# Expert results brought from columns back to rows by VectorE and a DRAM scratch in place of TensorE transposes

## The chip, the cores and the metric

The kernel runs on one core of a Trainium2 chip. Its engines work beside each other, each through its own queue in order: TensorE (PE, with its weight loads as PEld), VectorE (DVE), ScalarE (ACT), GpSimd (POOL) and SyncE (SP, which here only issues DMAs). The metric is the device time of one execution in microseconds, 367.65 us in the median of three runs of the kernel before.

## The reference

The input is q, k, v and forget logits of 4 sequences with 8 heads of 768 steps and 48 values. A gated linear attention comes first, then a mixture of 8 experts, of which each token uses one:

```python
f = 1.0 / (1.0 + np.exp(-f_logit))
for t in range(S):
    state = f[:, :, t, :, None] * state + np.einsum('bhd,bhe->bhde', k[:, :, t], v[:, :, t])
    y[:, :, t] = np.einsum('bhd,bhde->bhe', q[:, :, t], state)
x = y.transpose(0, 2, 1, 3).reshape(B * S, H * D)          # 3072 tokens of 384
logits = x @ w_gate
e_idx = np.argmax(logits, axis=1)
gate_w = softmax(logits)[np.arange(N), e_idx]
eom = 1.0 / (1.0 + np.exp(-(x @ w_output_gate)))
for e in range(E):                                         # 8 experts, 384 -> 1024 -> 384
    mask = e_idx == e
    ye = np.maximum(x[mask] @ w1[e], 0.0) @ w2[e]
    out[mask] = gate_w[mask, None] * eom[mask, e, None] * ye
```

## The kernel before

The first 126 us compute the attention, route each token and scatter its row of 384 values, with its number and 16 gate values behind it, into a DRAM list of its expert. What follows is the class `Experts`. The experts are taken by falling number of tokens, with capacities of 512, 448, 432, 416, 400, 400, 384 and 376 tokens, and are called expert 0 to 7 by that order.

Per expert, `mm1` (line 768) computes the hidden layer in eight f-steps of 128 hidden units: nine matmuls each, three input slices times three terms, since each factor is split into a high and a low part (`xh`, `xl`, `w1h`, `w1l`). ScalarE takes relu of the sum in PSUM as `hh` (line 783), and VectorE computes the rest `hl` from the same PSUM tile (line 784). This tile `h_ps` has two buffers, so f-step f+2 waits for `hl` of f-step f. `mm2` (line 791) is the second product. For experts 0 to 5 it has the weights of w2 stationary and the tokens as moving columns, so its result `y_ps` has the 384 output values on partitions, in three banks. `y_out` (line 822) copies the banks to SBUF, and `put` (line 829), called at f-steps 1 to 4 of the next expert's first product, turns one tile of 128 tokens by three TensorE transposes, lets ScalarE scale it by the token's gain and has POOL scatter the rows to the output by an indirect DMA. Experts 6 and 7, with three token tiles, use `mm2_rows` (line 805): there the tokens are stationary and w2 moves in 384 columns, so the result already has tokens on partitions. Expert 0 is done in two halves of 256 tokens, the first of them before the routing is known for all.

The order of the work on each compute engine is the order of the program, tied by `chain` (line 1086). So `run` (line 879) writes by hand what stands between the f-steps: the split of w2 into `w2h` on ScalarE and `w2l` on VectorE at even f-steps of the first product (line 632), and in the second product the splits of the next expert's w1, its three input slices (`x_in`, line 737: block transposes of 32 x 32 on VectorE, then `xh` and `xl`) and the thirteen small operations that compute the gains from the gate values `xm` (`gain_ops`, line 697). SP loads by expert: w1, the token blocks `xb`, `xm`, then w2 (lines 612 to 630 and 672), where each load waits for the split that frees its buffer.

Of the kernel before, what the change touches and what calls it, by code (L numbers as in the profile page):

```python
# [579 lines left out]
class Experts:  # L580
# [4 lines left out]
    def __init__(self, tc, nc, k, r, raw, right, w1, w2, xs_dram, out, kp):  # L585
        self.tc, self.nc, self.k, self.r, self.raw, self.right, self.kp = tc, nc, k, r, raw, right, kp
        self.w1, self.w2, self.xs, self.out = w1, w2, xs_dram.rearrange("(e n) w -> e n w", e=E), out
        k.gain = kp.tile([TS, NT, E], F32, name="gain")
        k.dst = kp.tile([TS, NT, E], I32, name="dst")

        self.first = kp.tile([TS, NT, RW], F32, name="first_x")
        self.apart, self.cleared, self.number = [], [], {}
        self.wr, self.whl, self.todo, self.gq = {}, {}, [], []
        self.xg, self.xb, self.xt, self.hs, self.ys, self.ysb = {}, {}, {}, {}, {}, {}
# [27 lines left out]
    def load_rest(self, s):  # L622
        e = self.number[s]
        if s > 0:
            self.blocks_in(s)
        for i in range(KF // 2):
# [5 lines left out]
    def split(self, m, s, i, eng=None):  # L632
        flat = lambda a: a.rearrange("p a b -> p (a b)")
        t = self.wr.pop((m, s, i))
        shape = [128, KC, 256] if m == 1 else [128, 2, DM]
        hi = self.wp.tile(shape, F32R, name=f"w{m}h")
        lo = self.wp.tile(shape, F32R, name=f"w{m}l")
        self.nc.scalar.copy(out=flat(hi), in_=flat(t))  # L638
        (eng or self.nc.vector).tensor_tensor(out=flat(lo), in0=flat(t), in1=flat(hi.bitcast(F32)), op=ALU.subtract)  # L639
        self.whl[m, s, i] = (hi, lo)  # L640


# [29 lines left out]
    def blocks_in(self, s):  # L672
# [7 lines left out]
        m = self.xp.tile([TS, NT, RW - DM], F32, name="xm")  # L680
# [3 lines left out]
        self.xb[s] = t[:, 0:nb, :]  # L684
        self.meta = getattr(self, "meta", []) + [(s, 0, nt, m)]

    def gains(self):

        kp = self.kp
        for s, j0, j1, t in self.meta:  # L690
            n = j1 - j0
            d, up, dn = (kp.tile([128, NT, E], F32, name=m)[:, 0:n] for m in ("g_d", "g_up", "g_dn"))
            mx, sm, so = (kp.tile([128, NT], F32, name=m)[:, 0:n] for m in ("g_mx", "g_sm", "g_so"))
# [3 lines left out]
    def gain_ops(self, s, j0, j1, t, d, up, dn, mx, sm, so):  # L697
# [4 lines left out]
        mine = k.perm[:, s, :] if s > 0 else self.r.top  # L702
        return [
            lambda: nc.gpsimd.tensor_scalar(out=k.dst[:, j0:j1, s], in0=t[:, 0:n, 0], scalar1=0.0,
# [86 lines left out]
    def mm2(self, s, f, part=0):  # L791

        wh, wl = self.whl[2, s, f // 2]
        hh, hl = self.hs[s, f][part]
        c0, n = sum(h[0].shape[1] for h in self.hs[s, f][:part]), hh.shape[1]
        for d in range(KC):
            if f == 0 and part == 0:
                self.ys[d] = self.psy.tile([128, 512], F32, name=f"y_ps{d}")
            ds = slice(d * 128, d * 128 + 128)
# [5 lines left out]
    def mm2_rows(self, s, step):  # L805

        k, nc = self.k, self.nc
        for j, n in self.rows(s):
            ps = self.psy.tile([128, 512], F32, name=f"y_ps{j}")
            i = 0  # L810
            for f in range(KF):
                wh, wl = self.whl[2, s, f // 2]
                hh, hl = (t[:, j * TS:j * TS + n] for t in self.hs[s, f][0])
                for a, b in ((hh, wh), (hl, wh), (hh, wl)):
                    nc.tensor.matmul(ps[0:n, 0:DM], a, b[:, f % 2, :], start=(i == 0), stop=(i == 3 * KF - 1))
                    i += 1
                step(j * KF + f)
            t = self.yp.tile([TS, DM], F32, name="o", bufs=3)
            nc.scalar.activation(out=t[0:n], in_=ps[0:n, 0:DM], func=AF.Copy, scale=k.gain[0:n, j, s:s + 1])
            self.scatter(s, j, n, t)  # L820

    def y_out(self, s):
        for d in range(KC):
            t = self.yp.tile([128, max(CAPS)], F32, name=f"y{d}")
            copy = self.nc.vector.tensor_copy if d == 1 else self.nc.scalar.copy
            copy(out=t[:, 0:CAPS[s]], in_=self.ys[d][:, 0:CAPS[s]])
            self.ysb[s, d] = t

    def put(self, s, j, n):
        ps = self.pso.tile([128, KC, 128], F32, name="o_ps")  # L830
        for d in range(KC):
            self.nc.tensor.transpose(out=ps[0:n, d, :], in_=self.ysb[s, d][:, j * TS:j * TS + n],
                                     identity=self.k.ident)
        t = self.yp.tile([TS, DM], F32, name="o", bufs=3)
        self.nc.scalar.activation(out=t[0:n], in_=ps[0:n].rearrange("p a b -> p (a b)"), func=AF.Copy,  # L835
                                  scale=self.k.gain[0:n, j, s:s + 1])
        self.scatter(s, j, n, t)

    def scatter(self, s, j, n, t):
        self.nc.gpsimd.indirect_dma_start(  # L840
# [38 lines left out]
    def run(self):  # L879
# [7 lines left out]
        for s in range(E):  # L887
# [33 lines left out]
            for f in range(KF):  # L921
# [6 lines left out]
                if s == 1:  # L928
                    step(1)
# [221 lines left out]
```

## Time and profile before

| what | value |
|---|---|
| median of three runs | 367.65 us (367.51 to 368.71) |
| profiled execution: time / span | 368.0 / 366.3 us |
| TensorE busy | 351.9 us, 96% of the span |
| VectorE busy | 245.9 us, 67% |
| ScalarE busy | 198.1 us, 54% |
| POOL busy | 146.2 us, 40% |
| SP's DMA queue | 56.82 MB in 58048 packets |

The span runs from the first to the last instruction of the profiled execution; the time of that execution is 1.7 us longer. Times in a timeline count from the span's start. A duration is what one instruction took from its start to its end. Matmuls are pipelined: the next one starts before the last has ended, so the distance of two starts says what one costs TensorE. The words in brackets behind a row are the idle time of the engine ahead of it and what ended it. The granted clock is TensorE's, in tenths of full speed on the page and as a fraction in the windows.

### The profile page before, as it was taken

What the parts mean: (1) busy time and instruction counts of PE and PEld (TensorE: products, weight loads), DVE (VectorE), ACT (ScalarE), POOL (GpSimd) and SP (SyncE); (2) the same over time, 40 slices, a digit from 0 to 9 for tenths busy, and PEclk for the clock granted to TensorE, in tenths of its full rate; (3) what the DMA queues carried; (4) which work ended last, traced back from release to release, by engine and by line L of the source; (5) the groups of instructions that cost most, each with busy time, mean ns of one, the idle gap of its engine ahead of it and who ended that gap; (6) DMA issues with size and microseconds to landing.
All of it is one profiled execution on the core that took longest, in us unless ns stands there. A gap on an engine that the chain in (4) does not pass through costs nothing. (4 is left out here: it accounts for less than half of the span.)

```text
span 366.3 us, 8386 instructions
## 1 busy us (share of the span) xinstructions
PE 351.9 (96%) x3121; PEld 327.0 (89%) x3121; DVE 245.9 (67%) x503; ACT 198.1 (54%) x468; POOL 146.2 (40%) x176
## 2 busy tenths in 40 slices
PE   8899999999998999999999999999999999999993
PEld 3678998888887899997999999999999999999993
DVE  6998989888994665666684585585575575666600
ACT  3576766866764652436634653554654654654510
POOL 6586796999989762001300220310210220242012
PEclk9999999999998999999999999999999999999999
DMA  8999999999548515976456456467366366331001
GB/s 258 348 359 356 338 223 257 297 262 252 174 121 269 206 74 158 254 244 150 136 177 125 168 180 134 137 192 160 129 197 154 129 196 154 131 103 58 2 23 43
DMA packets 61410, 67.09 MB, mean 183 GB/s; under 512 B 19106, under 2 KB 55989, under 8 KB 61360
## 3 DMA queue, kind: packets, MB, share of 16 engines
q1 hardware_dynamic: 58048, 56.82, 56.1%
q0 software_dynamic: 3312, 9.65, 7.3%
q8 instruction: 26, 0.43, 0.5%
q14 instruction: 24, 0.20, 0.2%
HBM read 53.53 MB, written 13.39 MB: 183 GB/s over the span
## 5 line engine op out<-in xcount | busy, mean ns | idle before, releaser
L840 POOL DMA_INDIRECT out<-o,dst x30 | 31.0, 1033 | 172.9 <-ACT o L835 87.5
L784 DVE SCALAR_TENSOR_TENSOR hl<-h_ps,hh 128x256 fp32r<-128x256 f32 (+6 forms) x72 | 39.2, 546 | 49.8 <-ACT hh L783 49.5
L779 PE MATMUL h_ps<-xh,w1h 128*128 128x400 f32 (+6 forms) x192 | 67.5, 351 | 0.8 <-ACT xh L733 0.5
L779 PE MATMUL h_ps<-xl,w1h 128*128 128x400 f32 (+6 forms) x192 | 65.1, 339 | 0.2 <-DVE xl L734 0.2
L779 PE MATMUL h_ps<-xh,w1l 128*128 128x400 f32 (+6 forms) x192 | 65.0, 338 | 0.0
L783 ACT ACTIVATE hh<-h_ps 128x256 fp32r<-128x256 f32 (+6 forms) x72 | 34.8, 483 | 49.3 <-PE h_ps L779 47.7
L801 PE MATMUL y_ps<-hh,w2h 128*128 128x256 f32 (+4 forms) x168 | 55.8, 332 | 0.0
L801 PE MATMUL y_ps<-hh,w2l 128*128 128x256 f32 (+4 forms) x168 | 55.6, 331 | 0.0
L801 PE MATMUL y_ps<-hl,w2h 128*128 128x256 f32 (+4 forms) x168 | 55.6, 331 | 0.0
L779 PEld LDWEIGHTS h_ps<-xh,w1h 128*128 128x128 f32 x192 | 36.1, 188 | 2.0 <-ACT xh L733 0.9
L779 PEld LDWEIGHTS h_ps<-xl,w1h 128*128 128x128 f32 x192 | 36.2, 188 | 0.9 <-DVE xl L734 0.5
L779 PEld LDWEIGHTS h_ps<-xh,w1l 128*128 128x128 f32 x192 | 36.0, 188 | 0.5
L226 POOL TENSOR_TENSOR q_t<-q_t,p 128x512 f32<-128x512 f32 x24 | 30.6, 1275 | 8.5 <-DVE p L212 5.6
L639 DVE TENSOR_TENSOR w2l<-w2r,w2h 128x768 fp32r<-128x768 f32 x31 | 30.7, 991 | 4.1 <-ACT w2h L638 1.9
L801 PEld LDWEIGHTS y_ps<-hh,w2l 128*128 128x128 f32 x168 | 31.6, 188 | 0.4
L801 PEld LDWEIGHTS y_ps<-hh,w2h 128*128 128x128 f32 x168 | 31.6, 188 | 0.4
L801 PEld LDWEIGHTS y_ps<-hl,w2h 128*128 128x128 f32 x168 | 31.6, 188 | 0.4
L248 PE MATMUL a_ps<-q_t,k_t 64*128 64x128 f32 x384 | 28.3, 285 | 3.7 <-POOL k_t L223 2.1
L212 DVE TENSOR_TENSOR_SCAN p<-f_ps,start_p 128x511 f32<-128x511 f32 x22 | 28.0, 1273 | 3.7 <-ACT start_p L200 2.1
L639 DVE TENSOR_TENSOR w1l<-w1r,w1h 128x768 fp32r<-128x768 f32 x28 | 26.9, 960 | 4.0 <-ACT w1h L638 2.5
L248 PEld LDWEIGHTS a_ps<-q_t,k_t 64*128 64x128 f32 x384 | 23.6, 187 | 6.5 <-POOL k_t L223 2.5
L223 POOL TENSOR_TENSOR k_t<-k_t,i 128x512 f32<-128x512 f32 x21 | 27.0, 1285 | 4.2 <-DVE i L219 2.7
(176 smaller groups left out, 739.1 us busy)
## 6 DMA issues: line engine op xcount, KB each, us to landing
w1r<-in_w SPq DMA_DIRECT2D x32, 384.0 KB, 4.0
w2r<-in_w SPq DMA_DIRECT2D x32, 384.0 KB, 3.1
xs_dram<-empty SPq DMA_DIRECT2D x8, 401.0 KB, 11.8
f_t<-in_f SPq DMA_DIRECT2D x6, 512.0 KB, 3.9
q_t<-in_q SPq DMA_DIRECT2D x6, 512.0 KB, 9.4
k_t<-in_k SPq DMA_DIRECT2D x6, 512.0 KB, 9.6
v_t<-in_v SPq DMA_DIRECT2D x6, 512.0 KB, 8.9
v_t<-in_v SPq DMA_DIRECT2D x4, 768.0 KB, 14.5
```

The lines of the kernel that those rows point to most:

```text
L212: nc.vector.tensor_tensor_scan(out=flat(d["p"])[:, 1:n], data0=flat(d["f"])[:, 0:n - 1], data1=sp[:, 1:n], initial=sp[:, 0:1], op0=ALU.mul ...
L223: eng.tensor_tensor(out=k_t[i][:, :, sl], in0=k_t[i][:, :, sl], in1=d["i"], op=ALU.mult)
L226: nc.gpsimd.tensor_tensor(out=q_t[i][:, :, sl], in0=q_t[i][:, :, sl], in1=d["p"], op=ALU.mult)
L248: nc.tensor.matmul(aps[t][par][:, g, :], k_t[b % 2][r, g, sl], q_t[b % 2][r, g, sl], start=(g == 0), stop=(g == NP - 1))
L639: (eng or self.nc.vector).tensor_tensor(out=flat(lo), in0=flat(t), in1=flat(hi.bitcast(F32)), op=ALU.subtract)
L779: nc.tensor.matmul(ps[:, 0:n], a[:, c, cs], b, start=(i == 0), stop=(i == 3 * KC - 1))
L783: nc.scalar.activation(out=hi, in_=ps[:, 0:n], func=AF.Relu)
L784: nc.vector.scalar_tensor_tensor(out=lo, in0=ps[:, 0:n], scalar=0.0, in1=hi.bitcast(F32), op0=ALU.max, op1=ALU.subtract)
L801: self.nc.tensor.matmul(self.ys[d][:, c0:c0 + n], a[:, f % 2, ds], b, start=(f == 0 and i == 0 and part == 0), stop=(f == KF - 1 and i == ...
L840: self.nc.gpsimd.indirect_dma_start(out=self.out, out_offset=bass.IndirectOffsetOnAxis(ap=self.k.dst[0:n, j, s:s + 1], axis=0), in_=t[0:n] ...
```

## The change

Expert 0 computes its second product by rows. Its four token tiles use the three banks in turn, and ScalarE scales each tile out of its bank. Experts 1 to 5 keep tokens as columns, but the split of w2 permutes the output values, so that each 32 partitions of a bank hold one contiguous quarter of the row. VectorE then turns each bank by one instruction of 32 x 32 block transposes out of PSUM, scales all three by the gain, and SP writes the result in four DMAs to a DRAM scratch and reads it back with tokens on partitions; POOL scatters from there. These steps stand in the list `back`, one of which is taken per f-step of the next expert's first product (three transposes, scaling, store, an empty step, fetch, first scatter), the rest in its second product. The gains of experts 1 to 5 are computed on 32-token blocks, four times over in the partitions, so that `xm` is loaded by four DMAs, and the token numbers come by a load of their own (`who`). The loads of w2 are issued after f-step 5 in place of ahead of the first product. The three result banks are allocated once. The scatters to the output no longer wait for one another.

```diff
+        self.yps = [self.psy.tile([128, 512], F32, name=f"y_ps{d}") for d in range(KC)]
...
+        if m == 2 and self.turned(s):
+            shape = [128, KC, 2 * 128]
+            flat = lambda a: a.rearrange("p d (x j) -> p d x j", j=SB)
+            t = t.rearrange("p a w -> p (a w)").rearrange("p (x d j) -> p d x j", d=KC, j=SB)
...
+        raw = t if m == 2 and self.turned(s) else flat(t)
-        self.nc.scalar.copy(out=flat(hi), in_=flat(t))
-        (eng or self.nc.vector).tensor_tensor(out=flat(lo), in0=flat(t), in1=flat(hi.bitcast(F32)), op=ALU.subtract)
+        self.nc.scalar.copy(out=flat(hi), in_=raw)
+        (eng or self.nc.vector).tensor_tensor(out=flat(lo), in0=raw, in1=flat(hi.bitcast(F32)), op=ALU.subtract)
...
+        return s > 0 and len(self.rows(s)) > KC
...
+        if self.turned(s):
+            for b in range(128 // SB):
+                self.nc.sync.dma_start(
+                    out=m[SB * b:SB * b + SB, 0:nb, :],
+                    in_=self.xs[bass.ds(e, 1), 0:nb * SB, DM:RW].rearrange("o (a t) w -> t (o a) w", t=SB))
+            self.who[s] = self.xp.tile([TS, NT, 1], F32, name="who")
+            self.nc.sync.dma_start(
+                out=self.who[s][:, 0:nt, :],
+                in_=self.xs[bass.ds(e, 1), 0:nt * TS, DM:DM + 1].rearrange("o (j p) w -> p (o j) w", p=TS))
+            self.meta = getattr(self, "meta", []) + [(s, 0, nb, m)]
+            return
...
-                self.nc.tensor.matmul(self.ys[d][:, c0:c0 + n], a[:, f % 2, ds], b,
-                                      start=(f == 0 and i == 0 and part == 0), stop=(f == KF - 1 and i == 2),
-                                      skip_group_check=True)
...
+                self.nc.tensor.matmul(self.yps[d][:, 0:n], a[:, d, fs], b, start=(f == 0 and i == 0),
+                                      stop=(f == KF - 1 and i == 2), skip_group_check=True)
+    def mm2_row(self, s, j, n, f):
+        ps = self.yps[j % KC]
+        wh, wl = self.whl[2, s, f // 2]
+        part, c0 = (j * TS // EARLY, j * TS % EARLY) if s == 0 else (0, j * TS)
+        hh, hl = (t[:, c0:c0 + n] for t in self.hs[s, f][part])
+        for i, (a, b) in enumerate(((hh, wh), (hl, wh), (hh, wl))):
+            self.nc.tensor.matmul(ps[0:n, 0:DM], a, b[:, f % 2, :], start=(f == 0 and i == 0),
+                                  stop=(f == KF - 1 and i == 2))
...
+    def turn_back(self, s):
+        nb = -(-CAPS[s] // SB)
+        yt = self.yp.tile([128, SLOTS // SB, BW], F32, name="yt")
+        ys = self.yps
+        def turn(d):
+            self.nc.vector.transpose(out=yt[:, 0:nb, SB * d:SB * d + SB],
+                                     in_=ys[d][:, 0:nb * SB].rearrange("p (a j) -> p a j", j=SB))
+        ob = self.yp.tile([128, SLOTS // SB, BW], F32, name="ob")[:, 0:nb, :]
+        def scale():
+            self.nc.vector.tensor_tensor(out=ob, in0=yt[:, 0:nb, :],
+                                         in1=self.k.gain[:, 0:nb, s:s + 1].broadcast_to([128, nb, BW]), op=ALU.mult)
+        rows = self.yd[s]
+        def store():
+            for b in range(128 // SB):
+                self.nc.sync.dma_start(
+                    out=rows[0:nb * SB, BW * b:BW * b + BW].rearrange("(a t) w -> t a w", t=SB),
+                    in_=ob[SB * b:SB * b + SB])
+        t = self.yp.tile([TS, NT, DM], F32, name="yr")
+        full = CAPS[s] // TS
+        def fetch():
+            self.nc.sync.dma_start(out=t[:, 0:full, :], in_=rows[0:full * TS].rearrange("(j p) w -> p j w", p=TS))
+            if CAPS[s] % TS:
+                self.nc.sync.dma_start(out=t[0:CAPS[s] % TS, full, :], in_=rows[full * TS:CAPS[s]])
+        def put(j, n):
+            self.other_rows(self.nc.gpsimd.indirect_dma_start(
+                out=self.out, out_offset=bass.IndirectOffsetOnAxis(ap=self.k.dst[0:n, j, s:s + 1], axis=0),
+                in_=t[0:n, j, :], in_offset=None, bounds_check=N - 1, oob_is_err=False))
+        self.back = ([lambda d=d: turn(d) for d in range(KC)] + [scale, store, lambda: None, fetch]
+                     + [lambda j=j, n=n: put(j, n) for j, n in self.rows(s)])
+    def backs(self, n=1):
+        for _ in range(min(n, len(self.back))):
+            self.back.pop(0)()
+    def other_rows(self, i):
+        for other in self.results:
+            self.tc.declare_no_dep(i.ins, other.ins, reason="other tokens")
+        self.results.append(i)
...
-            self.mm2(0, f)
+            for j, n in self.rows(0)[0:EARLY // TS]:
+                self.mm2_row(0, j, n, f)
+        self.back = []
...
-                self.load(s + 1, self.k.number[0:1, s + 1:s + 2])
-            back = self.rows(s - 1) if s > 0 and len(self.rows(s - 1)) > KC else []
+                self.load(s + 1, self.k.number[0:1, s + 1:s + 2], rest=False)
+                self.blocks_in(s + 1)
...
-                if 1 <= f <= len(back):
-                    self.put(s - 1, *back[f - 1])
+                self.backs(1)
+                if f == 5 and s > 0 and s + 1 < E:
+                    self.load_w2(s + 1)
...
+            if not self.turned(s):
+                if s == 0:
+                    for j, n in self.rows(0)[0:EARLY // TS]:
+                        self.row_out(0, j, n)
+                def beside(i):
+                    self.backs(1)
+                    if front and (i % 2 if s == 0 else i % 3 == 1):
+                        front.pop(0)()
+                    else:
+                        self.gain(1)
+                self.mm2_rows(s, EARLY // TS if s == 0 else 0, beside)
+                while front:
                     front.pop(0)()
-                self.gain(2)
-                if s == 1:
-                    step(1)
+            else:
+                for f in range(KF):
+                    self.mm2(s, f)
+                    if front:
+                        front.pop(0)()
+                    self.gain(2)
+                    self.backs(2)
+                    if s == 1:
+                        step(1)
...
-            self.y_out(s)
+            self.backs(len(self.back))
+            if self.turned(s):
+                self.turn_back(s)
```

## Rows read from the trace of the kernel before

**Rows 1.** The page, part 1, and the granted clock of part 2.

```profile
PE 351.9 (96%) x3121; PEld 327.0 (89%) x3121; DVE 245.9 (67%) x503; ACT 198.1 (54%) x468; POOL 146.2 (40%) x176
...
PEclk9999999999998999999999999999999999999999
```

**Rows 2.** TensorE's timeline, expert 2: start, duration, line, operands, count.

```profile
195.63 0.36 PE L779 MATMUL h_ps<-xh,w1h 128*128 128x432 f32 x1
...
197.37 0.36 PE L779 MATMUL h_ps<-xh,w1h 128*128 128x432 f32 x1
...
199.11 0.49 PE L832 MATMUL o_ps<-ident,y 128*128 128x128 f32 x3
199.35 0.44 PE L779 MATMUL h_ps<-xh,w1h 128*128 128x432 f32 x1
...
201.19 0.49 PE L832 MATMUL o_ps<-ident,y 128*128 128x128 f32 x3
```

**Rows 3.** Groups by line and shape: busy us, mean ns, idle before.

```profile
L639 DVE TENSOR_TENSOR w2l<-w2r,w2h 128x768 fp32r<-128x768 f32 x31 | 30.7, 991 | 4.1 <-ACT w2h L638 1.9
...
L638 ACT CAST w2h<-w2r 128x768 fp32r<-128x768 f32 x32 | 26.5, 827 | 0.0
...
L832 PE MATMUL o_ps<-ident,y 128*128 128x128 f32 x57 | 9.5, 274 | 0.0
...
L784 DVE SCALAR_TENSOR_TENSOR hl<-h_ps,hh 128x448 fp32r<-128x448 f32 x8 | 5.0, 622 | 5.4 <-ACT hh L783 5.3
...
L742 DVE STREAM_TRANSPOSE xc<-xb 128x448 f32<-128x448 f32 x6 | 4.5, 749 | 0.0
...
L713 DVE RECIPROCAL g_dn<-g_dn 128x32 f32<-128x32 f32 x6 | 2.1, 344 | 0.0
...
L734 DVE TENSOR_TENSOR xl<-xc,xh 128x448 fp32r<-128x448 f32 x3 | 1.9, 625 | 1.9 <-ACT xh L733 1.9
```

**Rows 4.** Timeline of ScalarE, first group of expert 2.

```profile
197.57 0.53 ACT L783 ACTIVATE hh<-h_ps 128x432 fp32r<-128x432 f32 x1 [1.21 <-PE h_ps L779]
197.99 0.82 ACT L638 CAST w2h<-w2r 128x768 fp32r<-128x768 f32 x1
```

**Rows 5.** Timeline of VectorE, the same place.

```profile
198.13 0.61 DVE L784 SCALAR_TENSOR_TENSOR hl<-h_ps,hh 128x432 fp32r<-128x432 f32 x1 [2.28 <-ACT hh L783]
198.85 0.96 DVE L639 TENSOR_TENSOR w2l<-w2r,w2h 128x768 fp32r<-128x768 f32 x1
```

**Rows 6.** Windows: span, busy PE, PEld, DVE, ACT, POOL, clock, DMA share, GB/s.

```profile
155.57:164.02 8.45, 8.45 (x74) 8.45 (x73) 5.15 (x12) 3.42 (x8) 0.00 (x0) 1.00 0.70 238
195.63:210.91 15.28, 15.28 (x86) 14.57 (x84) 7.61 (x12) 9.03 (x16) 3.01 (x3) 1.00 0.52 136
```

**Rows 7.** Timeline of TensorE, expert 7's second product by rows.

```profile
349.57 0.34 PE L815 MATMUL y_ps<-w2h,hh 128*128 128x384 f32 x1
...
351.69 0.34 PE L815 MATMUL y_ps<-w2h,hh 128*128 128x384 f32 x1
```

**Rows 8.** Timeline of VectorE before expert 1's input is turned.

```profile
156.92 0.96 DVE L639 TENSOR_TENSOR w1l<-w1r,w1h 128x768 fp32r<-128x768 f32 x1 [0.30 <-DMA w2r<-in_w]
157.79 0.18 DVE L706 TENSOR_REDUCE g_mx<-xm 128x4 f32<-128x32 f32 x1
```

**Rows 9.** Timeline of TensorE, first group of expert 1.

```profile
165.03 0.36 PE L779 MATMUL h_ps<-xh,w1l 128*128 128x448 f32 x1
165.89 0.47 PE L779 MATMUL h_ps<-xh,w1h 128*128 128x448 f32 x1 [0.50 <-ACT xh L733]
166.55 0.47 PE L779 MATMUL h_ps<-xl,w1h 128*128 128x448 f32 x1 [0.19 <-DVE xl L734]
```

**Rows 10.** DMA issues of SP for expert 1.

```profile
148.86 1.71 SPq L681 DMA_DIRECT2D xm<-xs_dram  x1
```

**Rows 11.** Timeline of POOL at the same time.

```profile
155.10 0.25 POOL L704 TENSOR_SCALAR dst<-xm 128x4 int32<-128x4 f32 x1 [11.74 <-DMA xm<-xs_dram]
```

**Rows 12.** The page, part 3, SP's queue.

```profile
q1 hardware_dynamic: 58048, 56.82, 56.1%
```

More of the change, by code (lines that the diff above doesn't have):

```diff
@@ L622, in load_rest, with load_w2 @@
     def load_rest(self, s):
-        e = self.number[s]
         if s > 0:
             self.blocks_in(s)
+        self.load_w2(s)
+    def load_w2(self, s):
+        e = self.number[s]
         for i in range(KF // 2):
@@ L702, in gain_ops @@
         mine = k.perm[:, s, :] if s > 0 else self.r.top
+        number, nt = (self.who[s], len(self.rows(s))) if self.turned(s) else (t, n)
         return [
-            lambda: nc.gpsimd.tensor_scalar(out=k.dst[:, j0:j1, s], in0=t[:, 0:n, 0], scalar1=0.0,
+            lambda: nc.gpsimd.tensor_scalar(out=k.dst[:, 0:nt, s], in0=number[:, 0:nt, 0], scalar1=0.0,
                                             scalar2=float(BIG), op0=ALU.max, op1=ALU.min),
@@ L789, in mm1_early, with mm2 @@
         self.mm1(0, f, True)
-    def mm2(self, s, f, part=0):
+    def mm2(self, s, f):
         wh, wl = self.whl[2, s, f // 2]
-        hh, hl = self.hs[s, f][part]
-        c0, n = sum(h[0].shape[1] for h in self.hs[s, f][:part]), hh.shape[1]
+        hh, hl = self.hs[s, f][0]
+        n, fs = hh.shape[1], slice((f % 2) * 128, (f % 2) * 128 + 128)
         for d in range(KC):
-            if f == 0 and part == 0:
-                self.ys[d] = self.psy.tile([128, 512], F32, name=f"y_ps{d}")
-            ds = slice(d * 128, d * 128 + 128)
@@ L800, in mm2 @@
             for i, (a, b) in enumerate(((wh, hh), (wl, hh), (wh, hl))):
-                self.nc.tensor.matmul(self.ys[d][:, c0:c0 + n], a[:, f % 2, ds], b,
-                                      start=(f == 0 and i == 0 and part == 0), stop=(f == KF - 1 and i == 2),
-                                      skip_group_check=True)
[L805 to L833, printed above, removed]
+                self.nc.tensor.matmul(self.yps[d][:, 0:n], a[:, d, fs], b, start=(f == 0 and i == 0),
+                                      stop=(f == KF - 1 and i == 2), skip_group_check=True)
@@ L834, in put, with mm2_rows @@
         t = self.yp.tile([TS, DM], F32, name="o", bufs=3)
-        self.nc.scalar.activation(out=t[0:n], in_=ps[0:n].rearrange("p a b -> p (a b)"), func=AF.Copy,
+        self.nc.scalar.activation(out=t[0:n], in_=self.yps[j % KC][0:n, 0:DM], func=AF.Copy,
                                   scale=self.k.gain[0:n, j, s:s + 1])
         self.scatter(s, j, n, t)
+    def mm2_rows(self, s, j0, step):
+        for j, n in self.rows(s)[j0:]:
+            for f in range(KF):
+                self.mm2_row(s, j, n, f)
+                step((j - j0) * KF + f)
+            self.row_out(s, j, n)
@@ L916, in run @@
             self.gains()
-            if len(self.rows(s)) <= KC:
-                self.mm2_rows(s, lambda i: self.gain(1) if i % 3 != 1 else front.pop(0)() if front else None)
-                self.gain(len(self.gq))
-                continue
-            for f in range(KF):
-                for part in range(len(self.hs[s, f])):
-                    if not (s == 0 and part == 0 and f < AHEAD):
-                        self.mm2(s, f, part)
-                if front:
-                    front.pop(0)()
-                self.gain(2)
-                if s == 1:
-                    step(1)
+            if not self.turned(s):
[10 more added lines that the diff above has]
+                while front:
+                    front.pop(0)()
+            else:
+                for f in range(KF):
+                    self.mm2(s, f)
[5 more added lines that the diff above has]
+                        step(1)
             self.gain(len(self.gq))
-            self.y_out(s)
+            self.backs(len(self.back))
+            if self.turned(s):
+                self.turn_back(s)
             if s == 0:
@@ L1089, in tile_kernel @@
     y_dram = dram.tile([H, D, N], F32, name="y_dram")
+    yd = [dram.tile([SLOTS, DM], F32, name=f"yd{s}") for s in range(E)]
     kp = ctx.enter_context(tc.tile_pool(name="const", bufs=1))
@@ L1096, in tile_kernel @@
         right = cx.enter_context(ExitStack())
-        ex = Experts(tc, nc, k, r, raw, right, w1, w2, xs_dram, out, kp)
+        ex = Experts(tc, nc, k, r, raw, right, w1, w2, xs_dram, out, kp, yd)
         with ExitStack() as c1:
```

24 lines of the change are left out of this document (14 added, 10 removed).

## The prediction

> **What bounds the kernel now.** I read the page first: TensorE is busy 96% of the span at a granted clock of 0.9 in all slices but one [rows 1], so what matters is what stands in its queue, and where it waits. The timeline of TensorE in expert 2's first product comes next [rows 2]. Eight groups of nine matmuls follow one another every 1.74 us (195.63 to 197.37). Where three transposes of the previous expert's result stand between two groups, the spacing is 2.08 (199.11 to 201.19): 0.24 for the transposes, and 0.10 more because the group's first matmul starts late. So a transposed row tile costs TensorE 0.34 us, and no wait is hidden in it. The whole-run groups [rows 3] give the prices of VectorE and ScalarE, and two timelines [rows 4, 5] show how an f-group hands over to them. The windows by stage [rows 6] show that VectorE has room in expert 2's first product (7.6 of 15.3 us busy), but not how that room lies, which decides this change.
>
> **What goes.** Experts 0 to 5 have four row tiles each, so 24 tiles with three transposes (57 full ones in [rows 3], the rest narrower ones at the same price): 24 x 0.34 = 8.2 us of the critical engine. This is at most 8.6 and at least 24 x 0.24 = 5.8, if the late first matmul stays. The ScalarE copies and scalings that go with them were beside TensorE and give nothing by themselves.
>
> **Expert 0 by rows.** Its second product was 144 matmuls of 256 columns, 8.45/72 = 0.117 us apiece [rows 6]. It becomes 96 of 384 columns, which experts 6 and 7 already do at (351.69 - 349.57)/12 = 0.177 [rows 7]: 16.9 becomes 17.0 in the second-half price, while the first half ran at 0.120. I take a gain of 0.1 (between -0.4 and +0.2).
>
> **What comes to VectorE in the first product of experts 2 to 6.** In f-steps 0 to 2 one block transpose each of 448 or 416 columns, in step 3 one scaling of 14 x 96 = 1344 or 13 x 96 = 1248 elements. A block transpose of 448 from SBUF takes 0.749 [rows 3]; I take 0.75 (0.70 for 416). The scaling is priced on w2l, 0.99 in the mean and 0.96 when undisturbed for 768 elements [rows 3, 5], with (0.96 - 0.622)/(768 - 448) = 1.06 ns per further element from it and hl of 448 columns: 1.57 and 1.47 us. Bounds: the transpose 0.62 to 1.24 (one or two plain passes of hl's length), the scaling 1.4 to 3.
>
> VectorE is in order, and the next hl (the low half of the hidden values) stands behind these. PSUM has two buffers for the first product, so group f+2 can't start until hl of group f is done. Before, hl ended at 198.13 + 0.61 = 198.74, for a group due at 199.11: 0.37 us of slack only [rows 2, 5]. I follow the hand-over for expert 2 from the start of group 0, with these steps: ScalarE's hh starts 0.20 after a group's last issue slot and hl 0.56 later [rows 4, 5], w2h follows 0.42 behind hh and is ready after 0.86, and a VectorE instruction lets the next start 0.08 before its own end (156.92 to 157.79 for one of 0.96 [rows 8]); I allow 0.05 from hl to the group that it releases.
> Step 0: hl ends at 3.1, w2l runs 3.2 to 4.1, the transpose to 4.8. Step 1: hl waits for it and ends at 5.40; group 3 was due at 5.22 and starts at 5.45, 0.23 late. The transpose runs to 6.0, hl of step 2 to 6.6, w2l 6.7 to 7.6, the transpose to 8.3. Step 3: hl ends at 8.88, just in time for group 5 at 8.93; the scaling runs to 10.3. Step 4: hl ends at 10.89 and group 6, due at 10.67, starts 0.27 late. Then the lag is gone. That is 0.50 us. The same steps with the shorter spacings of experts 3 to 6 (9 x 0.187, twice 9 x 0.180, 9 x 0.174) give 0.63, 0.62, 0.62 and 0.76: together 3.1 us. With the cheapest values (0.62, 1.4) they give 1.7, with a transpose of 1.24 they give 9.5, with a scaling of 3 they give 10.0.
> [...]
>
> **The permuted split of w2.** w2h and w2l of experts 1 to 5 read their input in runs of 32 columns. The element count stays, so I see no gain; the dearest near row is the block transpose, which reads every third element and takes 0.749 against 0.622 for a plain pass of as many columns: 1.2 times [rows 3]. At 1.2 the stalls are 5.1, at twice the price 19.6 and 2.5 more in expert 1. I take 1.0, since runs of 32 are nearer to plain reading.
>
> **Gains on 14 columns in place of 4.** For experts 1 to 5 four VectorE operations per expert grow from 32 to 112 elements (0.08 each by the slope above), and the reciprocal from 0.344 to at most 1.2 in proportion [rows 3]; I take 0.8. Some 1.0 us per expert lies in the second product, where VectorE ends its part 2 us ahead of TensorE; covered for experts 2 to 5, and if that cover went it would cost up to 1 us each. For expert 1 it isn't covered: these operations now come to stand between its last xl (then about 165.9) and its first hl, 2.1 us of them, so hl ends near 168.7 with group 2 due at 168.35: +0.4 (0 to +1).
>
> **The start of expert 1.** TensorE waits there for xh and xl: group 0's matmuls start at 165.89 and 166.55 in place of about 165.23 and 166.1, 1.1 us in all [rows 9]. In the new order x_in 2 has five gain operations ahead of it in place of eight, but the split before it starts 1 us later, since two scalings of expert 0's rows go ahead on ScalarE. I get the last xl 0.5 us earlier: -0.4 (-1.1 to +1).
>
> **What is moved on SP.** The xm load becomes four of the same size plus a column of 4-byte elements. The old xm was issued at 148.86 and released POOL at 155.10 [rows 10, 11]; VectorE first reads it at 157.79 [rows 8]. The queue's packets cost 0.561 x 16 x 366.3/58048 = 0.057 engine-us each on average [rows 12], so 3 x 448 more packets take at most 4.8 us and less in proportion to bytes: landing between 155.4 and 160, while the first read is now due near 158.9. I take no cost; late by 1.1 at most by this, 2 if SP's issue of 1.71 repeats. In later experts the load is issued over 15 us ahead. The w2 loads go behind the store, some 5 us later than now, 15 us ahead of their use. Store, fetch and the scatters behind the fetch hold up SP and POOL alone; the next w1 loads behind the fetch have a first product's length of cover. The last of it, expert 5's, is out during expert 6, so the tail stays. The kept banks are free long ahead: expert s's transposes run at most 9 us into the next first product, whose second product writes them 5 us later.
>
> **Sum.** -8.2 + 3.1 - 0.1 + 0.4 - 0.4 = -5.2 us. The profiled execution took 368.0 (span 366.3), which becomes 362.8; it lay 0.35 above the median of 367.65, so the median becomes 362.4. What is late next is VectorE's hl in the first products.
>
> **Rivals.**
> A, the back transposes hide. For it: VectorE is busy only half of that stage [rows 6]. Against it: the slack of a single hl is 0.37. With 1.7 of stalls and the wait of expert 1 gone: -8.2 + 1.7 - 0.1 - 1.1 = -7.7, 359.9.
> B, VectorE becomes the bound and the kernel slower. The place is the first product, the price the permuted split at 1.5 times (1.44 on VectorE, 1.23 on ScalarE): my steps then give 10.3 us of stalls, and 0.7 in expert 1: -8.2 + 11.0 - 0.1 = +2.7, 370.3. It decides from a split of about 1.35 times, or a transpose of 1.15 us, on: 8 us of stalls. Against it are the rows on plain and strided reading [rows 3]. [...]
> C, the enlarged xm lands late for expert 1 and VectorE, in order, holds x_in behind it: +2 us, 364.4. For it: DMA queues are the only thing with no cover there; against it the sum of packets.
> D, the two shares cancel: with a split at 1.2 times and a transpose of 1.0 the steps give 8.7 of stalls: -8.2 + 8.7 - 0.1 + 0.4 - 0.4 = +0.4, 368.0.
>
> **Chances.** My forecast 0.62 (its own range 360.5 to 364.7), A 0.12, C 0.06, D 0.07, B 0.13. About 0.3% (1.1 us) is what a measurement of this kernel tells from no change. Faster: 0.62 + 0.12 + 0.06 = 0.80; same 0.07; slower 0.13. The range 359.3 to 367.5 leaves out B, most of D and a little of A.
>
> **What would show it.** Right: no transposes by identity in the first products; spacing of 1.74 in expert 2 apart from two late groups released by hl, some 0.2 us each; block transposes near 0.75 and a scaling near 1.5 on VectorE; w2l still 0.96. Wrong: w2l or w2h above 1.2 us, block transposes above 1 us, a wait of VectorE for xm before 160, or TensorE idle in second products.

## The result, and the profile of the changed kernel

The changed kernel takes 361.61 us in the median of four runs (361.12 to 366.17), against 367.75 for the kernel before on the same chip: 0.985 of its time (95% interval 0.981 to 0.989), or 6.1 us less. The forecast was 362.4, with 5.2 us less. The profiled execution took 361.12 us, with a span of 359.4 against 366.3.

The page of the changed kernel, part 1 and the granted clock, answers to [rows 1]:

```profile
PE 343.4 (96%) x3001; PEld 317.6 (88%) x3001; DVE 259.4 (72%) x517; ACT 183.2 (51%) x436; POOL 146.8 (41%) x176
...
PEclk9999999999999999999999999999999999999999
```

A 9 on the clock's line stands for 0.9 or more, and not for 0.9 as the prediction reads it: the windows below, before and after, have 1.00 in every stage.

TensorE has 120 instructions and 8.5 us of work less, VectorE 13.5 us more. TensorE's share of the span stays at 96%, so the page doesn't yet say whether the new VectorE work is hidden. The windows do, if one cuts them at the first matmul of each stage. For the first products of experts 1 to 6, the changed kernel (columns as in [rows 6]):

```profile
163.01:178.87 15.86, 15.22 (x73) 13.37 (x73) 10.76 (x21) 7.88 (x14) 2.79 (x3) 1.00 0.78 189
193.41:207.81 14.40, 14.40 (x73) 13.28 (x72) 9.95 (x15) 6.61 (x11) 0.00 (x0) 1.00 0.61 97
221.73:235.79 14.06, 14.05 (x73) 13.21 (x72) 9.79 (x15) 6.52 (x11) 0.94 (x1) 1.00 0.61 135
249.23:262.91 13.68, 13.66 (x73) 12.95 (x73) 9.45 (x15) 6.43 (x11) 1.01 (x2) 1.00 0.61 137
276.03:289.71 13.68, 13.66 (x74) 12.94 (x73) 9.46 (x15) 6.44 (x11) 1.86 (x2) 1.00 0.63 155
302.86:316.18 13.32, 13.23 (x74) 12.43 (x74) 9.27 (x15) 6.35 (x11) 0.45 (x1) 1.00 0.46 116
```

The kernel before, the same stages but for expert 2, which stands in [rows 6]:

```profile
164.02:181.09 17.07, 16.38 (x86) 14.56 (x85) 10.68 (x21) 10.15 (x18) 3.01 (x3) 1.00 0.63 165
...
224.83:239.63 14.80, 14.80 (x86) 14.46 (x85) 7.45 (x12) 8.93 (x16) 3.01 (x3) 1.00 0.54 143
253.07:267.57 14.50, 14.50 (x85) 14.14 (x84) 7.27 (x12) 8.84 (x16) 3.01 (x3) 1.00 0.58 151
280.72:295.23 14.51, 14.51 (x86) 14.13 (x86) 7.27 (x12) 8.82 (x16) 3.02 (x3) 1.00 0.57 150
308.38:322.38 14.00, 14.00 (x86) 13.62 (x86) 7.03 (x12) 8.80 (x16) 3.04 (x3) 1.00 0.57 150
```

Every first product is 0.7 to 1.2 us shorter (the second number of a row is its length). Cutting the whole trace in this way gives the ledger below. "Front" runs from the span's start to expert 0's first product, "tail" from expert 7's second product to the span's end. The last columns are experiments that are told further down.

| us | before | expert 0 alone | changed | back at once | late gains | all three |
|---|---|---|---|---|---|---|
| front | 126.22 | 126.87 | 125.45 | 127.43 | 129.42 | 128.58 |
| expert 0 | 37.80 | 37.55 | 37.56 | 37.55 | 37.61 | 37.57 |
| first product, expert 1 | 17.07 | 15.05 | 15.86 | 16.21 | 14.86 | 14.41 |
| first products, experts 2 to 6 | 73.09 | 73.17 | 69.14 | 66.17 | 69.12 | 66.16 |
| second products, experts 1 to 6 | 80.92 | 80.91 | 80.88 | 81.19 | 80.87 | 80.89 |
| first product, expert 7 | 12.36 | 12.37 | 12.38 | 12.38 | 12.37 | 12.35 |
| experts, sum of the five above | 221.24 | 219.05 | 215.82 | 213.50 | 214.83 | 211.38 |
| tail | 18.84 | 18.78 | 18.13 | 18.27 | 18.15 | 18.24 |

So 5.42 of the profiled 6.9 us came from the experts, where the prediction looked for it: 0.24 in expert 0, 1.21 in the first product of expert 1, 3.95 in those of experts 2 to 6. The other 1.5 are 0.8 of front and 0.7 of tail. The experts' sum repeats to 0.03 us: 221.24, 221.22 and 221.21 in three traces with the order of before, 215.82, 215.81 and 215.84 in three of the changed kernel. The front doesn't: it ran from 125.45 to 132.63 in the three traces of one and the same changed kernel. The diff changes none of its work, so I count its spread as one between executions and not as an effect of the change; its cause wasn't tried. Sizes below 1 us are read from the experts' sum.

What is late now? TensorE's timeline of the changed kernel, expert 2's first product, of every three matmuls the first (`xh,w1h`; the two between are left out), around the late groups, answers to [rows 2]:

```profile
198.05 0.36 PE L806 MATMUL h_ps<-xh,w1h 128*128 128x432 f32 x1
198.70 0.46 PE L806 MATMUL h_ps<-xh,w1h 128*128 128x432 f32 x1
199.39 0.36 PE L806 MATMUL h_ps<-xh,w1h 128*128 128x432 f32 x1
...
203.51 0.36 PE L806 MATMUL h_ps<-xh,w1h 128*128 128x432 f32 x1
204.22 0.47 PE L806 MATMUL h_ps<-xh,w1h 128*128 128x432 f32 x1
204.91 0.36 PE L806 MATMUL h_ps<-xh,w1h 128*128 128x432 f32 x1
```

Undisturbed, three matmuls take 0.58. Group 3 starts at 198.70, which is 0.65 behind, and its next mark comes 0.69 later; group 6 at 204.22 has 0.71 and 0.69. So each late group costs twice: 0.07 and 0.13 of waiting, and 0.11 more because the matmul behind the wait takes longer to get going (0.46 in place of 0.36). The other 0.06 of what expert 2 loses lies in a slower start at group 5, 0.25 in place of 0.19 between two matmuls. Counted in the same way through experts 2 to 6, the late groups are groups 3 and 6 in each: 1.5 us of waiting in all, 1.1 behind the ten waits, and some 0.3 in small pieces, mostly at group 5. VectorE's timeline beside it shows what they waited for:

```profile
197.51 0.65 DVE L859 STREAM_TRANSPOSE yt<-y_ps 128x448 f32<-128x448 f32 x1
198.08 0.57 DVE L811 SCALAR_TENSOR_TENSOR hl<-h_ps,hh 128x432 fp32r<-128x432 f32 x1
198.57 0.63 DVE L859 STREAM_TRANSPOSE yt<-y_ps 128x448 f32<-128x448 f32 x1
...
202.11 1.54 DVE L865 TENSOR_TENSOR ob<-yt,gain 128x1344 f32<-128x1344 f32 x1
203.57 0.60 DVE L811 SCALAR_TENSOR_TENSOR hl<-h_ps,hh 128x432 fp32r<-128x432 f32 x1
```

`hl` of step 1 stands behind the first transpose and ends at 198.65, 0.05 ahead of group 3; `hl` of step 4 stands behind the scaling and ends at 204.17, 0.05 ahead of group 6. The prices, by the groups of the changed kernel (columns as in [rows 3]):

```profile
L650 DVE TENSOR_TENSOR w2l<-w2r,w2h 128x768 fp32r<-128x768 f32 x31 | 30.6, 989 | 3.5 <-ACT w2h L649 1.8
L649 ACT CAST w2h<-w2r 128x768 fp32r<-128x768 f32 x32 | 26.6, 830 | 0.0
...
L859 DVE STREAM_TRANSPOSE yt<-y_ps 128x416 f32<-128x416 f32 x9 | 5.4, 605 | 0.0
L811 DVE SCALAR_TENSOR_TENSOR hl<-h_ps,hh 128x448 fp32r<-128x448 f32 x8 | 5.0, 623 | 4.0 <-ACT hh L810 3.7
L769 DVE STREAM_TRANSPOSE xc<-xb 128x448 f32<-128x448 f32 x6 | 4.6, 772 | 0.0
L865 DVE TENSOR_TENSOR ob<-yt,gain 128x1248 f32<-128x1248 f32 x3 | 4.3, 1439 | 0.0
L859 DVE STREAM_TRANSPOSE yt<-y_ps 128x448 f32<-128x448 f32 x6 | 3.8, 639 | 0.0
L865 DVE TENSOR_TENSOR ob<-yt,gain 128x1344 f32<-128x1344 f32 x2 | 3.1, 1540 | 0.0
...
L740 DVE RECIPROCAL g_dn<-g_dn 128x112 f32<-128x112 f32 x2 | 1.7, 844 | 0.0
```

The four loads of `xm` for expert 1 were in time: VectorE's first read of it, answering to [rows 8], has no wait ahead of it:

```profile
157.69 0.26 DVE L733 TENSOR_REDUCE g_mx<-xm 128x14 f32<-128x112 f32 x1
```

### The profile page after: what moved, and what is told of

Read it like the earlier page. It is cut to its first block, busy times and chain, and to the rows that moved or that the text cites. A ratio compares the mean times of both kernels' runs of the same rounds, so it can differ in the third digit from the quotient of the medians.

```text
span 359.4 us, 8283 instructions
## 1 busy us (share of the span) xinstructions
PE 343.4 (96%) x3001; PEld 317.6 (88%) x3001; DVE 259.4 (72%) x517; ACT 183.2 (51%) x436; POOL 146.8 (41%) x176
## 3 DMA queue, kind: packets, MB, share of 16 engines
q1 hardware_dynamic: 78096, 63.76, 63.8%
## 5 line engine op out<-in xcount | busy, mean ns | idle before, releaser
L885 POOL DMA_INDIRECT out<-yr,dst x20 | 21.5, 1074 | 133.8 <-DMA yr<-yd 86.3
L825 PE MATMUL y_ps<-hh,w2h 128*128 128x400 f32 (+3 forms) x120 | 42.2, 352 | 0.0
L825 PE MATMUL y_ps<-hh,w2l 128*128 128x400 f32 (+3 forms) x120 | 42.1, 351 | 0.0
L825 PE MATMUL y_ps<-hl,w2h 128*128 128x400 f32 (+3 forms) x120 | 42.1, 351 | 0.0
L219 DVE TENSOR_TENSOR_SCAN i<-f_ps,start_i 128x512 f32<-128x512 f32 x22 | 26.9, 1223 | 0.8
L325 PE MATMUL x_ps<-turn,xt 128*128 128x112 f32 x192 | 25.7, 277 | 1.7 <-ACT xt L319 1.7
L649 ACT CAST w1h<-w1r 128x768 fp32r<-128x768 f32 x32 | 26.0, 834 | 2.3 <-POOL k_t L223 2.3
```

Of the source, the lines that this page charges most:

```text
L219: nc.vector.tensor_tensor_scan(out=flat(d["i"])[:, ::-1], data0=flat(d["f"])[:, ::-1], data1=flat(k.start_i[z])[:, ::-1], initial=0.0, op0 ...
L325: nc.tensor.matmul(xps[t][:, g, :], xt[t][:, g, :], turn[:, g, :], start=(g == 0), stop=(g == NP - 1))
L649: self.nc.scalar.copy(out=flat(hi), in_=raw)
L825: self.nc.tensor.matmul(self.yps[d][:, 0:n], a[:, d, fs], b, start=(f == 0 and i == 0), stop=(f == KF - 1 and i == 2), skip_group_check=True)
```

## The experiments

All comparisons below are with runs of the kernel before on the same chip. Expert 0 alone, the turn at once and the transposes twice ran on one chip (kernel before 369.66 us), expert 1's gains late, no round trip and all three on a second (369.81), the last four on a third (370.54). The changed kernel ran again on the first two.

**The changed kernel again.**

> The changed kernel once more beside the others, as their yardstick. Both theories: 361.6 us in the median (361.1 to 362.0), 6.0 us below the kernel before. The profile shown for it was 6.9 us below the profiled execution of before, of which 0.8 lies ahead of the experts and 0.7 behind the last scatter; if these two belong to the change, they are there again, and if they differ from run to run, the difference of medians stays near 5.4 to 6.

> The changed kernel once more, as the measure for the runs beside it. Theory: 5.5 to 6.5 us under the kernel before on the same chip (6.1 and 6.4 so far).

It took 0.983 (0.980 to 0.986) of the time of before on the first chip and 0.988 (0.984 to 0.992) on the second: 6.4 and 4.3 us less in the medians (363.26 and 365.49). The first is 0.4 more than expected, on a chip where both kernels were slower than in the first runs. The second misses its range; in its profile the experts gave the same 215.84 and the front had 132.63. That execution was the slowest of its six (368.65), and the others left no trace, so that the front made the miss is likely and not shown. From run to run, then, the change is worth 4.3 to 6.4 us in the medians, and 5.4 in the experts in each of the three traces. Of the 0.8 in the front and the 0.7 in the tail, the front's was not there again on the first chip (126.59, against 126.22 in the trace of before); of the tail's, 0.5 was (18.30).

**Expert 0 by rows, alone.** On the kernel before, the core of the edit:

```diff
-            self.mm2(0, f)
+            for j, n in self.rows(0)[0:EARLY // TS]:
+                self.mm2_row(0, j, n, f)
...
-            back = self.rows(s - 1) if s > 0 and len(self.rows(s - 1)) > KC else []
+            back = self.rows(s - 1) if s > 1 and len(self.rows(s - 1)) > KC else []
...
-            if len(self.rows(s)) <= KC:
+            if s == 0 or len(self.rows(s)) <= KC:
```

> The kernel before with expert 0's second product by rows alone; experts 1 to 5 keep TensorE's transposes. Theory (a transposed tile costs TensorE 0.34 us, VectorE's lateness is the only price): four tiles go, -1.36, the first half's shorter matmuls give -0.3, no block transpose or enlarged gain work is added, and TensorE's wait at expert 1's start may shrink by up to 0.5: 1.6 to 2.2 us below before, 365.6 to 366.1. Rival (the gain comes from the scratch path, the independent scatters and the moved loads): no change within 0.5 us, 367.2 to 367.8.

Measured: 0.995 (0.992 to 0.998), 2.45 us less in the medians, which is above my range, and 2.19 in the experts, at the range's upper end. The rival, no change, falls. Its windows, expert 0's early half of the second product and expert 1's first product:

```profile
137.54:146.53 8.99, 8.99 (x56) 8.96 (x55) 5.46 (x15) 2.52 (x6) 2.11 (x2) 1.00 0.52 158
164.42:179.47 15.05, 14.86 (x73) 13.44 (x73) 9.96 (x20) 7.85 (x14) 3.00 (x3) 1.00 0.69 176
```

The early half took 9.30 before. The window of expert 1's first product has 73 of TensorE's instructions in place of 86 (twelve transposes are gone), and it is 2.02 us shorter: 1.38 for the four transposed tiles at 0.346 apiece (below), 0.64 of waiting at its start. The whole changed kernel has 15.86 here: what else it adds at this place takes back 0.81, more than the 0.64.

**The turn at once.** The three transposes and the scaling go directly behind the second product, ahead of the next first product's first `hl`:

```diff
                 self.turn_back(s)
+                self.backs(4)
```

> The changed kernel with the three block transposes and the scaling of an expert right behind its second product, in place of f-steps 0 to 3 of the next first product; store, fetch and scatters follow one per f-step. Theory (hl waits behind these four instructions): VectorE stands idle 3.2 us there until the first hh (192.5 to 195.9 in expert 2), the work of 3.3 us begins 1 us before the second product ends, so the late groups 3 and 6 of experts 2 to 6 disappear, 2.7 us in sum, and at most 0.3 comes back in a late first hl: 358.9 to 359.4. Rival (those groups are late for ScalarE's hh or for a signal, not for VectorE's queue): no change, 361.2 to 361.9.

Measured: 0.976 (0.973 to 0.979), 8.9 us less than before and 2.5 less than the changed kernel in the medians of one chip. The first products of experts 2 to 6 fall from 69.14 to 66.17. Expert 2's, by its window:

```profile
196.07:210.00 13.93, 13.93 (x74) 13.51 (x73) 9.73 (x14) 6.61 (x11) 0.00 (x0) 1.00 0.97 223
```

TensorE needs 72 x 0.1934 = 13.92 here for 432 columns (1.74 for nine, [rows 2]); no group is late any more. VectorE's work in the stage is nearly the same (9.73 us against 9.95); what differs is its place. So the late groups cost 69.14 - 66.17 = 2.97, and without them the transposes' removal alone is 73.09 - 66.17 = 6.92 in five experts, 0.346 per tile.

**The transposes twice.**

```diff
-        self.back = ([lambda d=d: turn(d) for d in range(KC)] + [scale, ...
+        self.back = ([lambda d=d: (turn(d), turn(d)) for d in range(KC)] + [scale, ...
```

> The changed kernel with each of the 15 block transposes issued twice. Theory: the hand-over worked out in the prediction, with the measured prices (0.64 and 0.605 us a transpose, 1.54 and 1.44 the scaling), gives 2.5 us of stalls for the changed kernel and 9.1 with twice the transposes, so +6.6 us: 368 (366.8 to 368.8), the added time in groups 3 to 7 of experts 2 to 6. Rival (VectorE has room, busy 72% of the span): 15 x 0.55 = 8.3 us more of its work cost less than 1.5 us, 361.5 to 363.

Measured: 1.0035 (1.0014 to 1.0055), 7.4 us over the changed kernel; the first products of experts 2 to 6 grow from 69.14 to 76.57. 15 further transposes are 9.2 us of VectorE (3.8 + 5.4 in the groups above); four fifths of it arrive on the critical path, though VectorE is busy only 11.69 of 15.87 us in expert 2's window:

```profile
194.58:210.45 15.87, 14.74 (x74) 13.22 (x72) 11.69 (x18) 6.62 (x11) 0.00 (x0) 1.00 0.54 88
```

The rival, that idle time absorbs them, falls. The theory's +6.6 (5.2 to 7.2 by its range) was a little low.

**Expert 1's gains late.**

```diff
             for f in range(KF):
                 self.mm1(s, f)
+                if s == 1:
+                    self.gain(2)
...
-                    else:
+                    elif s > 0:
                         self.gain(1)
...
-            self.gain(len(self.gq))
+            if s > 0:
+                self.gain(len(self.gq))
```

> The changed kernel, with expert 1's thirteen gain operations taken out of expert 0's second product and taken two per f-step in expert 1's own first product. Theory (2.1 us of them stand between the last xl and the first hl of expert 1, and others ahead of its first x_in): 0.6 to 1.0 us under the changed kernel, group 2 of expert 1 and the two waits at its start released without delay. Rival (the start of expert 1 waits for the loads or for the row scalings on ScalarE): within 0.2 us of it.

Measured: 0.985 (0.982 to 0.989), against 0.988 (0.984 to 0.992) for the changed kernel on that chip: 1.2 us between the medians, with intervals that overlap. The ledger decides: expert 1's first product takes 14.86 in place of 15.86, and nothing else moves by more than 0.05. Not all waits are gone, as I had expected: 0.45 stay at the wait for the last `xl`. In the changed kernel VectorE had this between the last `xl` and the first `hl`:

```profile
164.44 0.62 DVE L761 TENSOR_TENSOR xl<-xc,xh 128x448 fp32r<-128x448 f32 x1 [0.63 <-ACT xh L760]
164.98 0.26 DVE L738 TENSOR_REDUCE g_so<-g_d 128x14 f32<-128x112 f32 x1
165.16 0.84 DVE L740 RECIPROCAL g_dn<-g_dn 128x112 f32<-128x112 f32 x1
...
167.30 0.62 DVE L811 SCALAR_TENSOR_TENSOR hl<-h_ps,hh 128x448 fp32r<-128x448 f32 x1
```

and TensorE waited for it in group 2, behind the wait for `xl` in group 0:

```profile
165.12 0.47 PE L806 MATMUL h_ps<-xl,w1h 128*128 128x448 f32 x1 [0.19 <-DVE xl L761]
...
167.97 0.47 PE L806 MATMUL h_ps<-xh,w1h 128*128 128x448 f32 x1 [0.38 <-DVE hl L811]
```

**No round trip.** The changed kernel without the store, the fetch and the scatters of experts 1 to 5, whose output rows are left out:

```diff
         self.back = ([lambda d=d: turn(d) for d in range(KC)] + [scale, store, lambda: None, fetch]
-                     + [lambda j=j, n=n: put(j, n) for j, n in self.rows(s)])
+        self.back = ([lambda d=d: turn(d) for d in range(KC)] + [scale])
```

> The changed kernel without the store to the DRAM scratch, the fetch from it and the scatters of experts 1 to 5: their rows of the output are not written. The transposes and the scaling on VectorE stay. Theory (the round trip stands on SP, POOL and DMA queues alone, with cover): within 0.3 us of the changed kernel. Rival (20000 more packets and SP's longer queue delay the loads of weights and tokens): 1 us or more under it.

Measured: 0.987 (0.984 to 0.991), beside 0.988 for the changed kernel on that chip; the experts take 215.83, against 215.84. The rival falls. The way through DRAM, 11152 packets of SP's queue by the two pages (78096 and 66944), costs nothing that shows.

**All three.** The turn at once, expert 1's gains late, and expert 0's first two row scalings on ScalarE one step later, behind the first split of w1:

```diff
-                if s == 0:
-                    for j, n in self.rows(0)[0:EARLY // TS]:
-                        self.row_out(0, j, n)
...
+                    if s == 0 and i == 2:
+                        for j, n in self.rows(0)[0:EARLY // TS]:
+                            self.row_out(0, j, n)
```

> The changed kernel with the back transposes and the scaling directly behind the second product, expert 1's gain operations in its own first product, and expert 0's first two row scalings one step later, behind the first w1 split. Theory (VectorE-late groups cost 2.5, the start of expert 1 1.1): 3 to 4 us under the changed kernel, 9 to 10.5 under the kernel before. Rival (the wait at expert 1's start remains, as the loads or xh set it): 2.3 to 2.8 under the changed kernel, as with the transposes moved alone.

Measured: 0.974 (0.970 to 0.977) of before, 10.1 us less (359.72), and so faster than both kernels; 5.8 under the changed kernel in the medians, 4.44 by the experts' sum. Expert 1's first product and expert 2's, by its windows:

```profile
166.15:180.56 14.41, 14.41 (x74) 13.52 (x73) 10.17 (x22) 7.86 (x16) 1.44 (x3) 1.00 0.81 196
195.09:209.01 13.92, 13.92 (x73) 13.52 (x72) 9.79 (x14) 6.61 (x11) 0.00 (x0) 1.00 1.03 229
```

Both are 72 matmuls at the undisturbed spacing, 0.200 and 0.193: no wait is left in them. (That busy time equals length doesn't show it: so it did in the changed kernel, 14.40 of 14.40, where 0.48 was lost in small pieces.) It came out better than the 3 to 4 that I expected under the changed kernel: the late groups were worth 2.97, not 2.5, and the start of expert 1 1.45, not 1.1, since both of my figures left out the slow first matmul behind a wait (2.5 had also more waiting in it than the 1.5 there was).

**The scaling three steps later, and one step later.** In the changed kernel, with empty steps ahead of it in the list:

```diff
-        self.back = ([lambda d=d: turn(d) for d in range(KC)] + [scale, store, lambda: None, fetch]
+        self.back = ([lambda d=d: turn(d) for d in range(KC)] + [lambda: None] * 3
+                     + [scale, store, lambda: None, fetch]
```

> The changed kernel with the scaling in f-step 6 of the next first product in place of step 3; the same work, three steps later. Theory (the hand-over of hl to the group two later sets the end, and no group of the first product waits for hl of steps 6 and 7): 1.2 to 1.4 us under the changed kernel, the first products of experts 2 to 6 at 14.1, 13.8, 13.4, 13.4 and 13.0 us, group 6 of expert 2 on time and group 3 still late. Rival (VectorE's amount of work in the stage sets it): no change within 0.2.

```diff
+        self.back = ([lambda d=d: turn(d) for d in range(KC)] + [lambda: None, scale, store, lambda: None, fetch]
```

> The changed kernel with the scaling in f-step 4 in place of step 3; the same work, one step later, in a step that also has a w2 split. Theory (hand-over by step: w2l and the scaling stand together ahead of the next hl): 3.8 to 4.7 us above the changed kernel, first products of experts 2 to 6 each some 0.85 longer, group 7 of expert 2 the late one. Rival (VectorE's amount of work in the stage): no change within 0.2.

Measured: 0.984 (0.980 to 0.988) with the scaling in step 6, 0.997 (0.994 to 1.000) in step 4. In step 4 the first products of experts 2 to 6 take 73.89, 4.75 more than in step 3 with the same instructions (0.95 each; I had 0.85), and expert 2's late group is group 7, as expected. The rival, that only the amount of work counts, falls. TensorE's timeline of that kernel:

```profile
208.20 0.35 PE L806 MATMUL h_ps<-xh,w1l 128*128 128x432 f32 x1
209.40 0.46 PE L806 MATMUL h_ps<-xh,w1h 128*128 128x432 f32 x1 [0.85 <-DVE hl L811]
```

In step 6 they take 67.85, 1.29 less, as expected (14.16, 13.78, 13.48, 13.47, 12.96), but the kernel wasn't 1.2 faster: its experts take 216.81, 1.0 more than in the changed kernel. Two things ate it. Expert 7's first product grew from 12.38 to 13.95: its input is turned beside expert 6's second product, and VectorE reached the first `w1l` of it at 319.41 (2.66 into that product) against 317.62 (1.44 into it), because the scaling now stands ahead of it. First the changed kernel, then this one:

```profile
317.62 0.96 DVE L650 TENSOR_TENSOR w1l<-w1r,w1h 128x768 fp32r<-128x768 f32 x1
```

```profile
317.57 1.45 DVE L865 TENSOR_TENSOR ob<-yt,gain 128x1248 f32<-128x1248 f32 x1
318.94 0.55 DVE L811 SCALAR_TENSOR_TENSOR hl<-h_ps,hh 128x384 fp32r<-128x384 f32 x1
319.41 0.95 DVE L650 TENSOR_TENSOR w1l<-w1r,w1h 128x768 fp32r<-128x768 f32 x1
```

This lateness reaches the last input slice, for which expert 7's first group waits: 0.74 of the 1.57. The other 0.8 lies in groups 5 and 6. Group 6 waited for `hl` of group 4, and this for an `hh` that ScalarE began 0.9 later than it does behind a group elsewhere (339.07, where 0.20 behind the group's last slot would be 338.15):

```profile
339.07 0.49 ACT L810 ACTIVATE hh<-h_ps 128x376 fp32r<-128x376 f32 x1 [1.75 <-PE h_ps L806]
...
340.19 0.44 PE L806 MATMUL h_ps<-xh,w1h 128*128 128x376 f32 x1 [0.43 <-DVE hl L811]
```

What held ScalarE up there isn't shown. My expectation followed the hand-over in the first product and not into the stage behind it. The other thing is 0.7 us in expert 1, told at the end.

**The scatters, and the kernel before once more.** On the kernel before, the scatters to the output are declared independent of one another, as in the changed kernel:

```diff
+        for other in self.results:
+            self.tc.declare_no_dep(i.ins, other.ins, reason="other tokens")
+        self.results.append(i)
```

> The kernel before, with the scatters to the output declared independent of one another as in the changed kernel, and nothing else. Theory (a scatter that needn't wait for the ones before it ends the tail earlier): 0.4 to 0.7 us under the kernel before, and 18.2 in place of 18.8 from the start of the last second product to the end. Rival (the tail of the changed kernel was shorter by chance): within 0.2 of the kernel before, tail 18.8.

> The kernel before once more, for its trace beside the runs of this series. Theory (the experts' stages depend on the order of the work alone): 221.2 us from the first product of expert 0 to the second of expert 7, as in its first trace, within 0.1; from there to the end 18.8 us.

Measured: 0.999 (0.996 to 1.003); tail 18.85, beside 18.77 in the kernel before once more, whose experts took 221.22. My theory of the tail falls. By the last line of POOL's timeline and the span, first of the kernel before with free scatters (span 369.3), then of the changed kernel (span 359.4):

```profile
364.26 1.03 POOL L840 DMA_INDIRECT out<-o,dst  x1 [3.25 <-POOLq L1110]
```

```profile
355.08 1.03 POOL L903 DMA_INDIRECT out<-o,dst  x1 [3.25 <-POOLq L1186]
```

5.0 us lie behind the last scatter's start in the one, 4.3 in the other; in ten traces of the changed kernel and its variants it is 4.3 to 4.7, in four of before and its variants 5.0. Up to that start the tail is 13.8 us in all fourteen. So some 0.5 us of the result lies behind the last scatter's start, and what makes it stays open.

## Why the prediction was right

The forecast was 0.8 us above the median, its sum of -5.2 stands against -5.42 in the experts, and none of the rivals came. Step by step:

- **24 transposed tiles, -8.2.** Right: 0.346 per tile (6.92/20) against 0.34, -8.3 in all. That the matmul behind the transposes starts late was part of the price, and it went with them.
- **VectorE late in experts 2 to 6, +3.1.** Right in place and sum: 2.97, in groups 3 and 6 of expert 2, released by `hl`. But that the size was met is luck: errors cancel in it. The forecast was 3.1 of waiting, and only 1.5 of waiting came. Block transpose and scaling were priced 0.75 and 1.57 and took 0.639 and 1.540; with these, my steps still give 2.5, so the steps themselves are some 0.1 too long per late group. On the other side they held only the wait, and each of the ten late groups costs about 0.11 more for its slow first matmul, which the same prediction had read from [rows 2] for the transposes and not carried over: 1.1, and 0.3 in small pieces. For expert 2: predicted 0.23 + 0.27 of waiting, measured 0.07 + 0.13, twice 0.11, and 0.06 in a group between.
- **Expert 0 by rows, -0.1.** Mis-sized: -0.24, all of it in the early half (9.30 to 9.01), inside the bounds given.
- **Expert 1, +0.4 - 0.4.** Its waits at the start became shorter, and group 2 came late behind the gains, as said; the reciprocal took 0.844 against 0.8. Without any wait the stage takes 14.41, so waits there were 17.07 - 14.41 - 4 x 0.346 = 1.28 before and 1.45 after: +0.17 in place of 0. Of the 1.45, group 2 makes 0.64, where 0.4 was forecast, and the start the rest.
- **Permuted split, 0.** Right: `w2l` 989 ns against 991, `w2h` 830 against 827 [rows 3]. So B and D, which both needed it dear (or a transpose of 1 us and more), fall. This is the step on which the sign hung.
- **Kept at nothing: xm, the round trip, second products.** Right: VectorE took `xm` without a wait ahead of expert 1 (at 157.69), so C falls; the round trip taken out changes nothing; the second products take 80.88 against 80.92.
- **Not foreseen:** about 0.5 us of the tail.

A, that the transposes hide, falls by the 2.97 us that came back when the same work was moved. Instructions that read PSUM were no slower here than their like from SBUF, for 448 columns in the changed kernel: `hl` from PSUM takes 623 ns and `xl` from SBUF 624, the block transpose from PSUM 639 and the one that reads SBUF with a stride 772.

## What to carry to other kernels

Work given to an engine that is idle for half of a stage is priced where it stands in that engine's queue, by the hand-over that waits behind it: the same instruction of 1.5 us cost 0.26 us per expert more in step 3 than in step 6, and 1.2 more in step 4, while in step 6 it was late for the stage behind. Give such work the place where the engine has nothing else to do and the next hand-over is farthest, here directly behind the product that it turns, where VectorE stood idle for 3.15 us, and follow it into the stage behind. Count with each wait of TensorE the slow start behind it, here 0.11 us. Cut both traces at the first matmul of each stage: the sum of the stages here repeats to 0.03 us in the traces of one kernel, where whole runs scatter by several.

## What was not expected of the hardware

Matmuls of 448 columns ran at two rates at one and the same granted clock of 1.00. Expert 1's second product, the changed kernel and the turn at once:

```profile
178.87:193.41 14.54, 14.54 (x75) 13.46 (x73) 11.71 (x29) 5.84 (x11) 0.00 (x0) 1.00 0.46 143
```

```profile
181.19:196.07 14.88, 14.88 (x74) 13.42 (x73) 12.64 (x31) 5.84 (x11) 0.00 (x0) 1.00 0.49 146
```

The spacing is 0.200 us in the one and 0.207 in the other, through all of expert 1's first and second product, in two of the fourteen traces (the turn at once, the scaling in step 6). It cost 0.7 us there, which is why the ledger of the turn at once shows 2.3 us under the changed kernel where the late groups give 3.0. What sets the rate was not tried. It also bounds what the experts' sum can tell of a variant: a difference of 0.7 us can be this.
